# Raw weights of the second batch in two rings and split in pairs, with two sums cut in two steps, in an attention and expert kernel

## The chip, the cores and the metric

One core of a Trainium2 chip runs the whole program. The metric is device time in microseconds (us). The kernel before took 845.05 us (median of three runs, from 843.41 to 851.78); its profiled execution took 843.36 us, of which the span from the first to the last instruction is 841.6 us. Engines are called PE (matmul), PEld (its weight loads), DVE (VectorE), ACT (ScalarE), POOL (GpSimd) and SP (which issues nearly all transfers).

## What is computed

```python
# attention: local window of 16 plus one summary key and value per block of 32; 2 batches, 8 heads, 768 positions
x = attention(q, k, v).reshape(1536, 512)
# first network: 512 -> 2048 -> 512, with a slope alpha per hidden unit
h = x @ w_in
x = (maximum(h, 0) + alpha * minimum(h, 0)) @ w_out
# second network: 4 experts, 512 -> 1024 -> 512, weighted by normalized probabilities p
for e in range(4):
    h = maximum(x @ w1[e], 0)
    out += p[:, e:e + 1] * (h @ w2[e])
```

All of it is float32. Every matmul operand is split into a high part (rounded to PE's fp32r format by an ACT copy) and a low part (operand minus high part, one subtraction on DVE or POOL); a product is three matmuls: high times high, high times low, low times high.

## The kernel before

The program runs attention, then the first network, then the experts; the change touches the experts of the second batch alone. Expert work is cut into 16 **units** per batch, each of two blocks of 128 hidden units (`NQ = 16`), numbered `s` = 0 to 15 for the first batch and 16 to 31 for the second.

The first layer of a unit is a seven-product scheme for 2x2 blocks (`e_steps`, L663). In the order of the work the steps are p1, p2, p6, p5, p7, p4, p3, each of six matmuls with 384 columns. p1, p6, p7 and p4 accumulate in one PSUM tile `cb`, p5 and p3 in `cd`, p2 stands in `ca`. After p1, p6 and p7 an ACT copy saves `cb` (tiles `p` and twice `u`, L669), and the next step on `cb` waits for it: p7 can begin only when the copy `u` after p6 is done. p2 is followed by a DVE addition (`ca`, L696), an ACT high part (`gh`), a DVE low part (`gl`) and an ACT copy for later sums (L686), and these stand ahead of that copy `u` on ACT, which works in order.

The scheme needs sums of both operands. Those of the inputs of batch 1 are the **own sums** (`x_combine`, L608): the blocks B11, B21 and B22 are split first, then four subtractions per half `k` turn the buffer `acc` into T1 to T4 (`own_sums`, on POOL for the second batch), and T1 to T4 are split in turn (`xh`/`xl` for T1, `xeh`/`xel` for the rest). Those of the weights were made and stored in the first batch; a unit of the second batch fetches S1 to S4 ready-made (`e_fetch`) and loads only A11, A12 and A22 raw (`e_load_again`, L470, tile `rc`, 384 KB in two transfers). It splits them in two parts: A11 with A12 (128x512) and A22 (128x256), each one ACT copy and one POOL subtraction (`e_split`, L381). Tile `rc` has one buffer, in the ring `rb` that the second-layer weights of odd units of the first batch use as well.

The second layer of units 16 to 29 is also done by seven products over a pair of units (`l2_quad`), in 21 pieces of six matmuls with 256 columns (`l2q`). Its sums of first-layer results are made on DVE by `s_sums` (four operations per block `f`, tiles `ft`, `fr`, `fe`) and split by `s_split` on ACT and POOL. `paired` weaves a unit's steps with the pieces: its string gives the order, each dot being one piece. After each dot, one entry of `after` runs, into which `e_prep` of the next unit is put: `first` (A11 and A12 split), `last` (A22 split) and `load` (the load for the unit after that), at places given by `at`. Units 15 and below, and 31, go through `standard`.

PE and ACT keep the order in which the code is written; a scheduler orders DVE, POOL and SP. `tc.issue_after(x)` makes it place work behind instruction `x`.

Of the kernel before, what the change touches and what calls it, by code (L numbers as in the profile page):

```python
# [8 lines left out]
F32 = mybir.dt.float32  # L9
# [3 lines left out]
ALU = mybir.AluOpType  # L13
# [79 lines left out]
def kernel(  # L93
# [376 lines left out]
    def e_load_again(s):  # L470
        if s >= 2 * NQ:
            return
        q = s % NQ
        pw["a", s] = t = gp.tile([P, 3, 2 * P], F32, tag="rb", name="rc", bufs=1)
        nc.sync.dma_start(out=t[:, 0:2].rearrange("p a c -> p (a c)"), in_=wb_in[0, 2 * q])
        nc.sync.dma_start(out=t[:, 2], in_=wb_in[0, 2 * q + 1][:, 2 * P:])
# [124 lines left out]
    def x_split(b, name, kk, hi, lo, src):  # L601
        nc.scalar.activation(hi, src, AF.Copy)
        eng = nc.gpsimd if b and name in ("B11", "B21", "B22", "T1") else nc.vector
        eng.tensor_tensor(lo, src, hi.bitcast(F32), op=ALU.subtract)
        for i, k in enumerate(kk):
            xs[b, name, k] = (hi[:, i], lo[:, i]) if len(kk) > 1 else (hi, lo)

    def x_combine(b):  # L608
# [9 lines left out]
        def own_sums(k):  # L618
            b11, b12, b21, b22 = x[:, k, u1], x[:, k, u2], x[:, 2 + k, u1], x[:, 2 + k, u2]
            for y, p, q in ((b11, b12, b11), (b12, b22, b12), (b22, b22, b11), (b21, b21, b22)):  # L620
                (nc.gpsimd if b else nc.vector).tensor_tensor(y, p, q, op=ALU.subtract)
# [102 lines left out]

    def s_sums(s, f):
        a11, a12, a21, a22 = (field(s, n, f) for n in ("A11", "A12", "A21", "A22"))
        nc.vector.tensor_tensor(a22, a21, a22, op=ALU.add)
# [195 lines left out]
    with tc.manual_schedule(engines={mybir.EngineType.PE, mybir.EngineType.Activation}):  # L923
        left, keep = [], []
        l2 = l2_steps(len(units) - 1)[KD // 2:]
        own_at = {NQ - 2: own1, NQ - 1: late1}

        def standard(s, l2, left):
# [3 lines left out]
            if s == NQ - 1:  # L932
                for k in range(2):
                    own_sums(k)
# [9 lines left out]
        def paired(s, order, fill, after=(), at=(2, 6)):  # L944
            fetch, first, last, load = e_prep(s + 1)
            after = list(after) + [lambda: None] * (at[1] - len(after))
            after.insert(at[0], first)
            after[at[1]:at[1]] = [last, load]
# [3 lines left out]
            for x in order:  # L952
# [5 lines left out]
                if s % 2 and quad(s) and x in "43":  # L958
                    s_sums(s, int(x == "4"))
# [8 lines left out]
        for a in range(UA, UB, 2):  # L968
            q = l2_quad(a)
            if old is None:  # L970
                paired(a, "1.26.57...4...3", left + l2, [lambda: None] + last1, (3, 5))
# [4 lines left out]
            else:  # L976
                n = 13 - done
                paired(a, "1.2.6.5.7..4.3" if n == 7 else "1.2.6..5.7..4..3.", old[done:13], splits, (3, 8))
# [8 lines left out]
        paired(UB, "1..2..6...5..7...4...3...", old[done:], splits, (3, 9))  # L987
# [65 lines left out]
```

## Time and profile before

| | before |
|---|---|
| median of the runs (lowest to highest) | 845.05 us (843.41 to 851.78) |
| profiled execution | 843.36 us |
| its span | 841.6 us |
| PE busy | 817.6 us, 97% of the span |
| DVE busy | 608.9 us, 72% |
| ACT busy | 427.3 us, 51% |
| POOL busy | 300.0 us, 36% |
| granted PE clock | full in all of the span but its first slices |

A busy share is an average over stages. The first network ends and the experts begin near 340 us, and the second batch's first unit begins at 583.98 us. A stall is the time for which PE waits between two matmuls. Since matmuls overlap, the time from the start of one to the start of the next tells more than a busy share.

### The profile page before, as it was taken

To read this page: it belongs to the slowest core of one execution; us is meant where nothing else is said; L and a number is where in the kernel's file an instruction comes from. 1 tells how busy PE (TensorE), PEld (TensorE's weight loads), DVE (VectorE), ACT (ScalarE), POOL (GpSimd) and SP (SyncE) were. 2 spreads that over 40 slices of the span, in tenths; PEclk is the share of its full clock that TensorE was granted. 3 is DMA by queue.
4 is the path that set the end of the run, shared out by engine and by line. 5 is a ranking of instruction groups with operands and counts; after the bars stand their busy time and mean duration, and the time that the engine had idled before them with its cause. 6 is when DMAs were issued, how large, how long until landed. Compare 5 with 4: busy or idle time off the path is not lost.

```text
span 841.6 us, 14451 instructions
## 1 busy us (share of the span) xinstructions
PE 817.6 (97%) x5000; PEld 746.0 (89%) x5000; DVE 608.9 (72%) x1313; ACT 427.3 (51%) x1050; POOL 300.0 (36%) x267
## 2 busy tenths in 40 slices
PE   4899999999999999999999999999999999999998
PEld 3699999888888888988989989988899999999997
DVE  7998667999983447477687678685667677767765
ACT  5999995544442334454454454463353554455430
POOL 0000000000013100396796696699153453354330
PEclk9799999999999999999999999999999999999999
DMA  8999413333322100276785785788675766766621
GB/s 310 294 298 298 149 45 102 100 100 101 98 78 75 51 1 0 101 264 225 262 279 215 257 295 196 259 310 294 203 219 188 251 207 213 247 212 227 212 75 75
DMA packets 97496, 155.37 MB, mean 185 GB/s; under 512 B 9872, under 2 KB 48272, under 8 KB 97424
## 3 DMA queue, kind: packets, MB, share of 16 engines
q1 hardware_dynamic: 96848, 154.18, 56.0%
q8 instruction: 39, 0.64, 0.3%
q10 hardware_dynamic: 576, 0.28, 0.1%
q14 instruction: 33, 0.27, 0.1%
HBM read 106.71 MB, written 47.71 MB: 183 GB/s over the span
## 4 chain that ended last, share of the span: by engine, by line
PE 87%; ACT 5%; DMA 4%; DVE 2%; issue 1%; SPq 0%; POOL 0%; ACTq 0%; POOLq 0%
PE l L530 47%; PE cb L646 15%; PE l2q L766 12%; PE cd L646 7%; PE ca L646 3%; ACT sm L232 2%; ACT sm L251 1%; PE s L213 1%; PE pt L257 1%; PE xps L275 1%; DMA bl<-dt 1%; DMA kw<-in_kw 1%; DMA raw<-in_wa 1%; ACT ptb L152 1%; DMA q<-in_qh 1%
## 5 line engine op out<-in xcount | busy, mean ns | idle before, releaser
L385 POOL TENSOR_TENSOR w0l<-ra,w0h 128x256 fp32r<-128x256 f32 (+1 forms) x32 | 36.8, 1151 | 356.8 <-ACT w0h L384 356.8
L813 DVE SCALAR_TENSOR_TENSOR acc<-l,prob_sb,acc 128x512 f32<-128x512 f32 x101 | 74.9, 746 | 28.3 <-PE l L530 28.3
L777 DVE SCALAR_TENSOR_TENSOR acc<-l2q,prob_sb,acc 128x256 f32<-128x256 f32 x156 | 71.0, 478 | 31.3 <-PE l2q L766 29.6
L530 PE MATMUL l<-xh,w0h 128*128 128x512 f32 (+1 forms) x240 | 84.4, 352 | 0.1
L530 PE MATMUL l<-gh,w1h 128*128 128x512 f32 (+1 forms) x240 | 83.3, 350 | 0.0
L530 PE MATMUL l<-xl,w0h 128*128 128x512 f32 (+1 forms) x240 | 83.1, 346 | 0.0
L530 PE MATMUL l<-xh,w0l 128*128 128x512 f32 (+1 forms) x240 | 83.1, 346 | 0.0
L530 PE MATMUL l<-gh,w1l 128*128 128x512 f32 (+1 forms) x240 | 82.9, 347 | 0.0
L530 PE MATMUL l<-gl,w1h 128*128 128x512 f32 (+1 forms) x240 | 81.4, 347 | 0.0
L530 PE MATMUL l<-w1h,gh 128*128 128x512 f32 x192 | 75.5, 393 | 0.0
L530 PE MATMUL l<-w1l,gh 128*128 128x512 f32 x192 | 75.1, 391 | 0.0
L530 PE MATMUL l<-w1h,gl 128*128 128x512 f32 x192 | 75.0, 391 | 0.0
L385 POOL TENSOR_TENSOR w0l<-rc,w0h 128x512 fp32r<-128x512 f32 (+1 forms) x32 | 33.0, 1034 | 80.5 <-ACT w0h L384 66.5
L669 ACT ACTIVATE u<-cb 128x384 f32<-128x384 f32 x64 | 31.3, 490 | 49.2 <-PE cb L646 49.2
L555 DVE SCALAR_TENSOR_TENSOR l<-m,beta,l 128x512 f32<-128x512 f32 (+1 forms) x60 | 38.6, 645 | 23.8 <-ACT m L549 23.7
L549 ACT ACTIVATE m<-l 128x512 f32<-128x512 f32 (+1 forms) x60 | 30.7, 514 | 46.6 <-PE l L530 46.3
L530 PEld LDWEIGHTS l<-xh,w0h 128*128 128x128 f32 x240 | 45.4, 189 | 6.1 <-ACT ptb L152 0.3
L530 PEld LDWEIGHTS l<-gh,w1l 128*128 128x128 f32 x240 | 45.4, 189 | 5.6
L530 PEld LDWEIGHTS l<-gh,w1h 128*128 128x128 f32 x240 | 45.4, 189 | 5.6
L530 PEld LDWEIGHTS l<-xh,w0l 128*128 128x128 f32 x240 | 45.4, 189 | 5.6
L530 PEld LDWEIGHTS l<-xl,w0h 128*128 128x128 f32 x240 | 45.4, 189 | 5.6
L530 PEld LDWEIGHTS l<-gl,w1h 128*128 128x128 f32 x240 | 45.4, 189 | 5.5
(165 smaller groups left out, 2542.3 us busy)
## 6 DMA issues: line engine op xcount, KB each, us to landing
raw<-in_wa SPq DMA_DIRECT2D x32, 512.0 KB, 4.1
rb<-in_wb SPq DMA_DIRECT2D x16, 512.0 KB, 4.8
ra<-in_wb SPq DMA_DIRECT2D x32, 256.0 KB, 3.7
dt<-xh SPq DMA_DIRECT2D x28, 256.0 KB, 3.4
dt<-xl SPq DMA_DIRECT2D x28, 256.0 KB, 4.7
bh<-dt SPq DMA_DIRECT2D x28, 256.0 KB, 3.4
bl<-dt SPq DMA_DIRECT2D x28, 256.0 KB, 3.1
q<-in_qh SPq DMA_DIRECT2D x24, 256.0 KB, 4.8
```

Of the source, the lines that this page charges most:

```text
L152: nc.scalar.activation(dst, src, AF.Copy)
L213: nc.tensor.matmul(sp[:, u], q[:, u // 2, u % 2], kw[:, :, u // 2, u % 2], start=True, stop=True)
L232: nc.scalar.activation(sm[:, u], sm[:, u], AF.Exp, bias=mx[:, u:u + 1], scale=-1.0, accum_out=sume[:, u:u + 1],)
L385: nc.gpsimd.tensor_tensor(lo, src, hi.bitcast(F32), op=ALU.subtract)
L530: ins = nc.tensor.matmul(ps, a, c, start=(i == 0), stop=(i == n - 1))
L549: nc.scalar.activation(m, gs[i, c0][0], AF.Relu, scale=-1.0)
L555: nc.vector.scalar_tensor_tensor(ps, m, beta[:, i:i + 1], ps, op0=ALU.mult, op1=ALU.add)
L646: nc.tensor.matmul(ps, l, r, start=(first and i == 0), stop=(i == len(terms) - 1), skip_group_check=True)
L669: nc.scalar.activation(v[name], ps, AF.Copy)
L766: nc.tensor.matmul(ps, l, r, start=(first and j == 0), stop=(j == len(terms) - 1), skip_group_check=True)
L777: nc.vector.scalar_tensor_tensor(dst, ps, pe, dst, op0=ALU.mult, op1=ALU.add)
L813: nc.vector.scalar_tensor_tensor(acc2[:, t], ps, pe, acc2[:, t], op0=ALU.mult, op1=ALU.add)
```

## The change

It makes five edits. (1) The raw weights of unit 16 are loaded into the ring `raw` (three buffers); the other units keep the one buffer in `rb`. (2) Low parts of B11 and B21 of batch 1 go from POOL to DVE. (3) The own sums come in two steps: the three subtractions per half that make T1, T2 and T3 where all four stood, the one for T4 behind the low parts of T1. (4) In `paired`, A22's split and the next load follow in the gap right behind the split of A11 and A12, at an earlier place than before; unit 18 also has its second piece after p6 ahead of p5. (5) `s_sums` loses its first addition, now `s_first`, which is done at once; the other three for the block `f = 0` are done behind the low part that follows the next unit's p2.

```diff
@@ e_load_again
-        pw["a", s] = t = gp.tile([P, 3, 2 * P], F32, tag="rb", name="rc", bufs=1)
+        if s == NQ:
+            t = wp.tile([P, 3, 2 * P], F32, tag="raw", name="rc", bufs=3)
+        else:
+            t = gp.tile([P, 3, 2 * P], F32, tag="rb", name="rc", bufs=1)
+        pw["a", s] = t
@@ x_split
-        eng = nc.gpsimd if b and name in ("B11", "B21", "B22", "T1") else nc.vector
-        eng.tensor_tensor(lo, src, hi.bitcast(F32), op=ALU.subtract)
+        eng = nc.gpsimd if b and name in ("B22", "T1") else nc.vector
+        low = eng.tensor_tensor(lo, src, hi.bitcast(F32), op=ALU.subtract)
+        if b:
+            mark[name] = low.ins
@@ x_combine
-        def own_sums(k):
+        def own_sums(k, part=None):
             b11, b12, b21, b22 = x[:, k, u1], x[:, k, u2], x[:, 2 + k, u1], x[:, 2 + k, u2]
             for y, p, q in ((b11, b12, b11), (b12, b22, b12), (b22, b22, b11), (b21, b21, b22)):
-                (nc.gpsimd if b else nc.vector).tensor_tensor(y, p, q, op=ALU.subtract)
+                if part is None or part == (y is b21):
+                    (nc.gpsimd if b else nc.vector).tensor_tensor(y, p, q, op=ALU.subtract)
@@
+    def s_first(s, f):
+        nc.vector.tensor_tensor(field(s, "A22", f), field(s, "A21", f), field(s, "A22", f), op=ALU.add)
+
     def s_sums(s, f):
         a11, a12, a21, a22 = (field(s, n, f) for n in ("A11", "A12", "A21", "A22"))
-        nc.vector.tensor_tensor(a22, a21, a22, op=ALU.add)
         nc.vector.tensor_tensor(a21, a11, a21, op=ALU.subtract)
@@ the expert loops
-        own_at = {NQ - 2: own1, NQ - 1: late1}
+        def own_last():
+            with tc.issue_after(mark["T1"]):
+                for k in range(2):
+                    own_sums(k, True)
+
+        own_at = {NQ - 2: own1, NQ - 1: late1 + [own_last]}
@@ standard
             if s == NQ - 1:
                 for k in range(2):
-                    own_sums(k)
+                    own_sums(k, False)
@@ paired
-        def paired(s, order, fill, after=(), at=(2, 6)):
+        def paired(s, order, fill, after=(), at=1):
             fetch, first, last, load = e_prep(s + 1)
-            after = list(after) + [lambda: None] * (at[1] - len(after))
-            after.insert(at[0], first)
-            after[at[1]:at[1]] = [last, load]
+            after = list(after) + [lambda: None] * (at - len(after))
+            after[at:at] = [first, lambda: (last(), load())]
@@
                 if s % 2 and quad(s) and x in "43":
-                    s_sums(s, int(x == "4"))
+                    s_first(s, int(x == "4"))
+                    if x == "4":
+                        s_sums(s, 1)
+                elif x == "2" and s % 2 == 0 and s > UA:
+                    with tc.issue_after(mark[s, 0, 0]):
+                        s_sums(s - 1, 0)
@@
-                paired(a, "1.26.57...4...3", left + l2, [lambda: None] + last1, (3, 5))
+                paired(a, "1.26.57...4...3", left + l2, [lambda: None] + last1, 3)
...
-                paired(a, "1.2.6.5.7..4.3" if n == 7 else "1.2.6..5.7..4..3.", old[done:13], splits, (3, 8))
+                paired(a, "1.2.6..57..4.3" if n == 7 else "1.2.6..5.7..4..3.", old[done:13], splits, 3)
...
-        paired(UB, "1..2..6...5..7...4...3...", old[done:], splits, (3, 9))
+        paired(UB, "1..2..6...5..7...4...3...", old[done:], splits, 3)
```

POOL at the seam of the two batches, from the low part of S1 and S2 of unit 15 on (`w0l<-s`), before. `acc<-acc` is an own subtraction, `xl<-acc` the low part of an input block, `w0l<-rc` that of raw weights of units 16 and 17:

```order
L604 TENSOR_TENSOR xl<-acc,xh 128x2x384 x3
L385 TENSOR_TENSOR w0l<-s_6416,w0h 128x512
L385 TENSOR_TENSOR w0l<-ra,w0h 128x256
L385 TENSOR_TENSOR w1l<-rb,w1h 128x512
L621 TENSOR_TENSOR acc<-acc 128x384 x2
L385 TENSOR_TENSOR w1l<-rb,w1h 128x512
L621 TENSOR_TENSOR acc<-acc 128x384 x5
L385 TENSOR_TENSOR w0l<-rc,w0h 128x512
L385 TENSOR_TENSOR w0l<-rc,w0h 128x256
L621 TENSOR_TENSOR acc<-acc 128x384
L604 TENSOR_TENSOR xl<-acc,xh 128x384 x2
```

The same place now:

```order
L628 TENSOR_TENSOR acc<-acc 128x384 x2
L608 TENSOR_TENSOR xl<-acc,xh 128x2x384
L385 TENSOR_TENSOR w0l<-s_6416,w0h 128x512
L628 TENSOR_TENSOR acc<-acc 128x384
L385 TENSOR_TENSOR w0l<-ra,w0h 128x256
L385 TENSOR_TENSOR w1l<-rb,w1h 128x512
L628 TENSOR_TENSOR acc<-acc 128x384
L385 TENSOR_TENSOR w1l<-rb,w1h 128x512
L628 TENSOR_TENSOR acc<-acc 128x384 x2
L385 TENSOR_TENSOR w0l<-rc,w0h 128x512
L385 TENSOR_TENSOR w0l<-rc,w0h 128x256
L608 TENSOR_TENSOR xl<-acc,xh 128x384 x2
```

Ahead of unit 16's weights there stood seven own subtractions and three wide low parts, and there stand now six and one; the two subtractions for T4 follow behind the last row shown.

DVE around p2 of unit 18, before (`ca<-ca,p` is the addition after p2, `fr`, `fe` are sums of unit 17's results, `acc<-l2q` adds a piece of the second layer):

```order
L730 TENSOR_TENSOR fr<-fr,fe 128x384
L728 TENSOR_TENSOR fr<-fe,fr 128x384
L696 TENSOR_TENSOR ca<-ca,p_7025 128x384
L777 SCALAR_TENSOR_TENSOR acc<-l2q,prob_sb,acc 128x256
L729 TENSOR_TENSOR fe<-ft,fe 128x384
L681 SCALAR_TENSOR_TENSOR gl<-ca,gh 128x384
L730 TENSOR_TENSOR fr<-fr,fe 128x384
```

And now:

```order
L739 TENSOR_TENSOR fr<-fr,fe 128x384
L703 TENSOR_TENSOR ca<-ca,p_7022 128x384
L786 SCALAR_TENSOR_TENSOR acc<-l2q,prob_sb,acc 128x256
L688 SCALAR_TENSOR_TENSOR gl<-ca,gh 128x384
L737 TENSOR_TENSOR fr<-fe,fr 128x384
L786 SCALAR_TENSOR_TENSOR acc<-l2q,prob_sb,acc 128x256
L738 TENSOR_TENSOR fe<-ft,fe 128x384
```

One subtraction went from before the addition after p2, and one from before its low part, to behind that low part.

ACT from the end of unit 18 to the copy `u` after p6 of unit 19, before:

```order
L686 ACTIVATE ft<-cd 128x384
L734 ACTIVATE xh<-fr 128x384
L384 ACTIVATE w0h<-rc 128x256
L669 ACTIVATE p_7197<-cb 128x384
L680 ACTIVATE gh<-ca 128x384
L686 ACTIVATE fe<-ca 128x384
L384 ACTIVATE w0h<-rc 128x512
L669 ACTIVATE u_7248<-cb 128x384
```

And now:

```order
L693 ACTIVATE ft<-cd 128x384
L743 ACTIVATE xh<-fr 128x384 x2
L676 ACTIVATE p_7197<-cb 128x384
L687 ACTIVATE gh<-ca 128x384
L693 ACTIVATE fe<-ca 128x384
L384 ACTIVATE w0h<-rc 128x512
L384 ACTIVATE w0h<-rc 128x256
L676 ACTIVATE u_7255<-cb 128x384
```

The 128x256 copy ahead of `p` (unit 19's A22) has left this stretch for one behind p7 of unit 18; the one now ahead of `u` is unit 20's A22, whose 128x512 copy stood there before as well.

## Rows read from the trace of the kernel before

**Rows 1.** The page: span, then busy us (share) xinstructions of each engine.

```profile
span 841.6 us, 14451 instructions
PE 817.6 (97%) x5000; PEld 746.0 (89%) x5000; DVE 608.9 (72%) x1313; ACT 427.3 (51%) x1050; POOL 300.0 (36%) x267
```

**Rows 2.** Waits of PE, 350 to 841 us: us in total, times, longest.

```profile
PE cb L646 <- ACT u L669: 3.2, 3, 1.4
PE cb L646 <- POOL w0l L385: 0.7, 1, 0.7
PE cd L646 <- DVE gl L681: 0.3, 1, 0.3
```

**Rows 3.** Stretches, line 646: length, PE busy (x), PEld busy (x), clock, DMA share, GB/s.

```profile
568.47:575.77 7.30, 7.30 (x42) 7.14 (x41) 1.00 0.72 217
583.98:594.30 10.32, 8.14 (x42) 7.02 (x41) 1.00 0.72 263
```

**Rows 4.** Stretches, PE alone: length, PE busy (x), clock, DMA share, GB/s.

```profile
619.75:625.18 5.43, 4.84 (x33) 1.00 0.66 176
633.62:640.57 6.95, 5.57 (x38) 1.00 0.71 215
664.88:670.16 5.28, 5.28 (x39) 1.00 0.88 262
668.40:669.11 0.71, 0.71 (x7) 1.00 0.79 231
```

**Rows 5.** Timeline at the seam: start us, length us, instruction, [idle before <-releaser].

```profile
578.36 5.22 POOL L621 TENSOR_TENSOR acc<-acc 128x384 f32<-128x384 f32 x5
578.90 0.39 SPq L475 DMA_DIRECT2D rc<-in_wb  x1
583.11 0.94 ACT L384 ACTIVATE w0h<-rc 128x512 fp32r<-128x512 f32 x2 [5.43 <-DMA rc<-in_wb]
583.82 1.98 POOL L385 TENSOR_TENSOR w0l<-rc,w0h 128x512 fp32r<-128x512 f32 x2 [0.24 <-ACT w0h L384]
```

**Rows 6.** Chain of waits, 583 to 594.6 us: start us, us, what.

```profile
585.32 3.47 DVE xel L604 x3
...
590.55 0.48 DVE ca L696
...
592.62 0.49 ACT u L669
```

**Rows 7.** Timeline around unit 18's p2.

```profile
619.10 2.62 POOL L735 TENSOR_TENSOR xl<-ft,xh 128x384 fp32r<-128x384 f32 x2
619.47 1.37 DVE L728 TENSOR_TENSOR fr<-fe,fr 128x384 f32<-128x384 f32 x1
620.76 0.55 DVE L696 TENSOR_TENSOR ca<-ca,p 128x384 f32<-128x384 f32 x1
623.47 0.48 ACT L669 ACTIVATE u<-cb 128x384 f32<-128x384 f32 x1
```

**Rows 8.** Timeline in unit 19.

```profile
634.23 0.33 SPq L475 DMA_DIRECT2D rc<-in_wb  x1
635.28 0.49 ACT L686 ACTIVATE fe<-ca 128x384 f32<-128x384 f32 x1 [0.68 <-DVE gl L681]
638.33 0.63 ACT L384 ACTIVATE w0h<-rc 128x512 fp32r<-128x512 f32 x1 [2.56 <-DMA rc<-in_wb]
```

**Rows 9.** Line 604, low parts of inputs: ns min/median/max, first and last start, forms.

```profile
L604 DVE TENSOR_TENSOR xel<-acc,xeh x12: 550/556/1370, 324.8 to 597.1; 128x384 fp32r<-128x384 f32 x12
L604 DVE TENSOR_TENSOR xl<-acc,xh x5: 552/958/958, 300.1 to 328.9; 128x768 fp32r<-128x768 f32 x3, 128x384 fp32r<-128x384 f32 x2
L604 POOL TENSOR_TENSOR xl<-acc,xh x5: 1323/1840/1847, 566.6 to 588.3; 128x768 fp32r<-128x768 f32 x3, 128x384 fp32r<-128x384 f32 x2
```

**Rows 10.** Timeline in unit 17: its copy after p6 and its p7.

```profile
609.85 0.48 ACT L669 ACTIVATE u<-cb 128x384 f32<-128x384 f32 x1
610.98 0.33 PE L646 MATMUL cb<-xeh,wfh 128*128 128x384 f32 x1
```

## The prediction

> **What bounds the kernel now.** I read the page first. PE is busy for 817.6 of 841.6 us [rows 1], so other engines matter only where PE waits for them. The whole idle time is 24 us. Of it, only what lies in the expert stage, which begins behind 340 us, can be touched, and there the waits of PE [rows 2] are five in all, three of them for the ACT copy `u` that saves the PSUM tile between p6 and p7 (3.2 us), one for the low part of unit 16's raw weights (0.7), one for a DVE low part (0.3). Nothing else in that stage stops PE. So the change can give at most what these five stalls cost, and the rest of my work is to price each and ask whether its cause goes.
>
> A wait as listed is less than the cost of a stall, because matmuls overlap and the first after a pause runs longer. I therefore compare stretches with the same matmuls. Unit 15's seven steps take 7.30 us for 42 matmuls; the 42 from unit 16's p1 to its p7 (two steps of unit 15 among them) take 10.32 [rows 3]. The **seam** costs 3.02 us: the wait for the raw weights, the one for DVE and one for `u`. From p6 to the end of p7 unit 21 takes 5.28 us; unit 19, with the same steps and pieces, 6.95 [rows 4], so its stall costs 1.67. Unit 18 has one piece fewer in that stretch, and one takes 0.71, so 5.28 - 0.71 = 4.57 is due; it takes 5.43 and loses 0.86. Together 3.02 + 0.86 + 1.67 = **5.55 us** can be gained.
>
> **The seam, raw weights (edits 1 to 3).** Unit 16's load is issued at 578.90 and ACT gets it at 583.11 after 5.43 us of waiting [rows 5], since its one buffer belongs to unit 15's second-layer weights until POOL has split them. In the ring `raw` it takes a buffer last used by unit 14, which is a whole unit (583.98 - 568.47 = 15.5 us, rows 3) earlier: the wait of ACT goes. That alone is worth nothing, as POOL is late too: its five own subtractions end at 578.36 + 5.22 = 583.58, 0.24 before the low part starts [rows 5]. Now two wide low parts (1.84 each on POOL, rows 9) and one own subtraction (5.22 / 5 = 1.04) leave the queue ahead of it, 4.72 us, so POOL could start at 583.82 - 4.72 = 579.1.
>
> Against that stand waits between POOL and DVE. DVE's subtraction of two SBUF tiles takes 0.55 us alone and up to 1.37 [rows 9]; three took 3.47 while POOL ran [rows 6], 1.16 each. DVE gets two more of the wide kind (0.96 each, rows 9), and the four narrow ones come earlier, into POOL's busy time. If POOL stood still for all of them it would lose 2 x 0.96 + 4 x 0.55 = 4.1 us and start at 583.2; if for none, at 579.1. PE wants the low part with p1's third matmul, about 584.3, and it takes 1.3 of the 1.98 of both. Cost left: nothing to 0.2 us. I take nothing. The first own subtraction also waits for DVE's low part of B11, which falls in the same bounds.
>
> **The seam, p5 and p7 of unit 16.** p7 needs `u`, and ACT, in order, does `u` behind the work on p2's result, which starts with DVE's `ca`. That came at 590.55 because DVE was working on T2 and T3 (`xel`, 3.47 us from 585.32, when ACT's copies had come at last) [rows 6]. From the end of `ca` (591.03) to the end of `u` (593.11) are 2.08 us. Without stalls p2 ends three steps after 583.98, at 587.10 (a step is 7.30 / 7 = 1.04), and p7 is due three steps later, 3.12. So `ca`, 0.55 long [rows 7], must begin within 0.5 us of p2's end. ACT's copies of T2 and T3 now wait for the own subtractions alone, which end between 579.1 and 583.2; with 0.9 for two copies (0.94 in rows 5) the three `xel` run from 580 to 584 to 583.5 to 587.6, and additions to `acc` that queued behind them follow. At the early end DVE is free in time; at the late end most of the old loss stays. I take the middle, 581 for POOL, at which `ca` is just in time or some tenths late: 0.2 us left, between 0 and the 2.0 or so that the seam lost there (3.02 less the 0.7 of rows 2 and its slow restart).
>
> Here a rule speaks against the change. The rows just read show DVE's two-input subtractions more than doubled beside POOL. The Trainium skill (SBUF — State Buffer, "Who interferes with whom") says that a DVE instruction with two SBUF inputs and a GpSimd instruction that reads SBUF exclude each other for a whole instruction. By that rule none of the moved low parts is hidden under POOL's work, and the first rival below would be likelier than I make it; without it the first bound, 0, would stand.
>
> **Unit 18 (edit 5, and the piece ahead of p5).** `ca` came at 620.76, right behind a subtraction for the sums that took 1.37 while POOL ran; `u` ended at 623.95 [rows 7], and p7 was due at 619.75 [rows 4] + 2 x 1.04 + 2 x 0.71 = 623.25. That subtraction now stands behind `gl`, and so does the next. `ca` then moves up by between 0.55 (the subtraction alone; its slow part could pass to the one before) and 1.3 us, and `gl` by the next subtraction's 0.55 more at best: `u` ends between 622.1 and 623.4. Left: 0 to 0.15, I take 0. The piece ahead of p5 needs the low parts `xl<-ft` 1.04 us earlier; POOL finished them at 621.72 [rows 7], and its 128x256 low part no longer stands before them. PE comes to that piece at 621.50 and to the first low part two short matmuls later, so even at the old times it loses next to nothing. The sums of `f = 0` that come later feed pieces that are several steps off.
>
> **Unit 19 (edit 4).** ACT stood from 635.77 to 638.33 before the copy of unit 20's weights, with `u` behind it; the load was issued at 634.23, so it took 4.1 us [rows 8]. Its call now stands in unit 18 two pieces and two steps earlier, 2 x 0.71 + 2 x 1.04 = 3.5 us: issue at 630.7 or earlier, there at 634.8, 1 us before ACT wants it. Left: nothing to the whole 1.67; I take nothing.
>
> **What else moves.** In units of odd number A22's copy (128x256) now stands ahead of `u`, and in unit 17 the 128x512 copy too (0.63 us, rows 8). Unit 17 has the least cover: `u` ended at 610.33 and p7 began at 610.98 [rows 10], 0.65 of slack for 0.63; without it 0.1 us would be lost. Edit 4 issues no transfer more; unit 16's goes out earlier, among others that use the queue at a DMA share of 0.72 [rows 3]; nothing waits there within a microsecond. PE's own instructions are the same.
>
> **Sum.** 5.55 - 0.2 = 5.35 us off the profiled execution's 843.36: 838.0. Before, the median of the runs stands 1.7 above that execution, the lowest run at it; I put the median at **838.5 us**.
>
> **Rivals.**
> - *The port.* DVE and POOL hold each other up at the seam so that `ca` is as late as before. For it: rows 6 and 9. Against it: 4.72 us less in POOL's queue. 2 us of the gain stay out: 840 to 841.
> - *The load is early for nothing.* SP issues it late, or POOL alone decides: the whole seam stays, and units 18 and 19 gain 2.53: 841.
> - *Slower.* The one buffer for raw weights is now asked for earlier in every unit, and ACT, in order, meets its copies earlier. If the transfer is not there when ACT reaches it in an odd unit, `u` waits, as unit 19 showed for 1.67 us. It decides from the point where the transfer lands later than the copy `fe` ends; for unit 19 I found 1 us of room. Units 19 to 29 are six odd units with the same order: 838.0 + 6 x 1.67 = 848 us, slower than before. Against it: later units had no such stall, the load has moved up further than its use, and a transfer takes some 4 us where a unit takes 15.
> - *More than the five stalls.* PE would have to run the same matmuls faster; nothing in the change touches that.
>
> **Chances.** My forecast 0.65; the port 0.17; the early load for nothing 0.08; slower 0.05; other 0.05. The measurement of this kernel tells about 1% from no change, 8.4 us. My forecast, at 0.8%, is within it and so are all rivals; faster by more needs a median below 836.6, which takes all 5.55 us and lucky runs, 0.08; slower by over 1% needs more than the slower rival, 0.03; 0.89 for the rest. The range runs from 836.6 (all stalls gone, the runs close to the profiled one) to 842.3 (the port or the seam left as it is, with the runs' usual 1 to 2 us above the profiled execution).
>
> **What would show it.** Right: no wait of PE for `u` in units 18 and 19, the stretch from unit 16's p1 to its p7 near 7.5 us, ACT without a wait for `rc`, POOL's low part of unit 16's weights before 583. Wrong: `ca` of unit 16 starting over 0.5 us after p2's last matmul with `xel` or additions ahead of it; PE at p1 of unit 16 still waiting for POOL; a wait for `rc` on ACT in odd units; a wait at the piece ahead of p5 in unit 18.

## The result, and the profile after

| | before | after |
|---|---|---|
| median of 5 runs, us | 845.23 (843.41, 845.05, 845.23, 851.43, 851.78) | 838.82 (837.62 to 839.05) |
| profiled execution, us | 843.36 | 838.46 |
| its span, us | 841.6 | 836.7 |
| waits of PE behind 345 us | 4.2 | none |

The ratio is 0.9896 (0.9848 to 0.9944), which is that of the means of the five runs, 838.57 and 847.38 us. That is a gain of 1.04%, and its interval excludes no change. The medians differ by 6.41 us, 0.76%, where 0.8% was forecast, and the time lies 0.3 us from the forecast. With 0.89 on "within 1%", that part of the prediction failed.

Between the two profiled executions the steps did what the forecast said. These are stretches of line 653 (646 before) and of PE alone in the changed kernel; the columns are those of [rows 3] and [rows 4], and each stretch ends where the next matmul starts, as there.

```profile
584.59:591.90 7.31, 7.30 (x42) 7.14 (x41) 1.00 0.82 299
```

```profile
617.39:621.96 4.57, 4.57 (x33) 1.00 0.29 93
630.40:635.68 5.28, 5.28 (x39) 1.00 0.79 253
```

The 42 matmuls of the seam take 7.31 us after 10.32, p6 to p7 of unit 18 takes 4.57 after 5.43, and of unit 19 5.28 after 6.95. That is 3.01 + 0.86 + 1.67 = 5.54 us (forecast 5.35): all that the five stalls cost. The spans differ by 4.9 only, since the changed kernel's execution comes 0.65 us later to the first expert matmul, ahead of all that the change touches. Here it is before, then after:

```profile
336.19 0.33 PE L646 MATMUL cb<-xh,w0h 128*128 128x384 f32 x1
336.84 0.33 PE L653 MATMUL cb<-xh,w0h 128*128 128x384 f32 x1
```

From there to the end, the **expert part**, the execution before took 505.4 us and the one after 499.8. The timeline of the seam (start us, length us, instruction) answers to [rows 5] and [rows 6]:

```profile
578.20 0.92 ACT L384 ACTIVATE w0h<-rc 128x512 fp32r<-128x512 f32 x2
578.65 0.55 DVE L688 SCALAR_TENSOR_TENSOR gl<-c,gh 128x384 fp32r<-128x384 f32 x1
581.01 2.63 POOL L385 TENSOR_TENSOR w0l<-rc,w0h 128x512 fp32r<-128x512 f32 x2
582.06 3.29 DVE L608 TENSOR_TENSOR xel<-acc,xeh 128x384 fp32r<-128x384 f32 x3
...
587.94 0.57 DVE L703 TENSOR_TENSOR ca<-ca,p 128x384 f32<-128x384 f32 x1
...
590.11 0.49 ACT L676 ACTIVATE u<-cb 128x384 f32<-128x384 f32 x1
```

ACT no longer waits for `rc`. POOL starts on it at 581.01 (taken: 581). `ca` starts 0.2 after p2 gives way to the next step (587.74), and `u` is there 0.26 before p7 starts (590.86). For unit 19, against [rows 8], the load of unit 20's weights leaves at 625.47 (at 630.7 or earlier, said the forecast), and ACT finds it landed:

```profile
632.05 0.49 ACT L693 ACTIVATE fe<-ca 128x384 f32<-128x384 f32 x1 [0.68 <-DVE gl L688]
632.44 0.93 ACT L384 ACTIVATE w0h<-rc 128x512 fp32r<-128x512 f32 x2
633.27 0.48 ACT L676 ACTIVATE u<-cb 128x384 f32<-128x384 f32 x1
```

What the two traces do not explain is the comparison: its two runs of the kernel before above 851 us stand 6 to 8 us above its others, and there is no such stall in [rows 2]. Without these two the mean before would be 844.56 us and the gain 6.0 us, 0.7%.

### The profile page after: what moved, and what is told of

Read it like the earlier page. It is cut to its first block, busy times and chain, and to the rows that moved or that the text cites. A ratio compares the mean times of both kernels' runs of the same rounds, so it can differ in the third digit from the quotient of the medians.

```text
span 836.7 us, 14449 instructions
## 1 busy us (share of the span) xinstructions
PE 814.9 (97%) x5000; PEld 745.1 (89%) x5000; DVE 614.5 (73%) x1315; ACT 428.3 (51%) x1050; POOL 294.6 (35%) x265
## 4 chain that ended last, share of the span: by engine, by line
PE 92%; ACT 4%; DMA 2%; DVE 1%; issue 0%; ACTq 0%; SPq 0%
PE l L534 48%; PE cb L653 16%; PE l2q L775 13%; PE cd L653 8%; PE ca L653 4%; PE s L213 2%; ACT sm L232 1%; DMA kw<-in_kw 1%; ACT sm L251 1%; PE xps L275 1%; PE pt L257 1%; DMA alpha_sb<-in_alpha 1%; ACT ptb L152 1%; ACT xh L152 0%; ACT m L553 0%
## 5 line engine op out<-in xcount | busy, mean ns | idle before, releaser
L385 POOL TENSOR_TENSOR w0l<-s,w0h 128x512 fp32r<-128x512 f32 x32 | 47.9, 1515 | 2.9 <-ACT w0h L384 2.9
```

Source lines behind the costliest of these rows:

```text
L385: nc.gpsimd.tensor_tensor(lo, src, hi.bitcast(F32), op=ALU.subtract)
```

## The experiments

Behind each expectation stand the median in us and the ratio to the kernel before in the same comparison, with its 95% interval. There are five comparisons besides the one above. The kernel before had a median of 843.56 in the first comparison (24 runs), 843.06 in the second (35), 844.48 in the third (35), 843.24 in the fourth (17), 849.51 in the fifth (23).

### What each edit is worth

**Edits 1 to 3 taken back** (unit 16's `rc` from the one buffer, low parts of B11 and B21 on POOL, own sums in one step).

```
-        if s == NQ:
-            t = wp.tile([P, 3, 2 * P], F32, tag="raw", name="rc", bufs=3)
-        else:
-            t = gp.tile([P, 3, 2 * P], F32, tag="rb", name="rc", bufs=1)
-        pw["a", s] = t
+        pw["a", s] = t = gp.tile([P, 3, 2 * P], F32, tag="rb", name="rc", bufs=1)
...
-        eng = nc.gpsimd if b and name in ("B22", "T1") else nc.vector
+        eng = nc.gpsimd if b and name in ("B11", "B21", "B22", "T1") else nc.vector
...
-        own_at = {NQ - 2: own1, NQ - 1: late1 + [own_last]}
+        own_at = {NQ - 2: own1, NQ - 1: late1}
...
-                    own_sums(k, False)
+                    own_sums(k)
```

> The changed kernel with edits 1 to 3 taken back (unit 16's raw weights in their old ring, low parts of B11 and B21 on POOL, all own sums in one step); edits 4 and 5 stay. Theory (five separate stalls, each owned by its edits): the stretch from unit 16's p1 to the start of what follows its p7 is 10.3 us again and units 18 and 19 stay without a stall: the span is 3.0 us above the changed kernel's. Rival (the stalls are linked: what unit 16 loses is made up later or brings the others back): the span differs by under 1 us or over 4.5 us.

840.67; ratio 0.9963 (0.9947 to 0.9980). PE waited 0.4 us for `w0l` and 0.9 for one `u` at the seam, and nowhere else. The expert part takes 501.7 us, 1.9 more than in the changed kernel: less than the theory's 3.0 and more than the rival's 1, so neither holds as it stands.

**Edit 4 and the piece ahead of p5 taken back** (the same at the other calls of `paired`).

```
-            after[at:at] = [first, lambda: (last(), load())]
+            after.insert(at[0], first)
+            after[at[1]:at[1]] = [last, load]
...
-                paired(a, "1.2.6..57..4.3" if n == 7 else "1.2.6..5.7..4..3.", old[done:13], splits, 3)
+                paired(a, "1.2.6.5.7..4.3" if n == 7 else "1.2.6..5.7..4..3.", old[done:13], splits, (3, 8))
```

> The changed kernel with edit 4 taken back (places of the splits and of the load in the gaps, and the order of unit 18's piece and p5, as before). Theory: the load for unit 20 is issued some 9 us later, ACT waits 2 to 3 us for it in unit 19, the stretch from p6 to the end of p7 there is 6.95 us instead of 5.28 and the span is 1.7 us above the changed kernel's; unit 18 stays at 4.57. Rival (the sums alone, edit 5, cured both units): unit 19 stays at 5.28 and the span is the same.

839.39; 0.9960 (0.9940 to 0.9979). One wait of PE is left, 1.1 us for `u` of unit 19, behind ACT's wait for the load, as in [rows 8]. Unit 19's stretch takes 6.62 us (6.95 expected), and the expert part 1.4 us more than in the changed kernel (1.7 expected). One of the 12 runs took 848.40.

```profile
630.52 0.33 SPq L479 DMA_DIRECT2D rc<-in_wb  x1
```

```profile
634.31 0.63 ACT L384 ACTIVATE w0h<-rc 128x512 fp32r<-128x512 f32 x1 [2.27 <-DMA rc<-in_wb]
634.85 0.47 ACT L676 ACTIVATE u<-cb 128x384 f32<-128x384 f32 x1
```

**Edit 5 taken back.**

```
-                    if x == "4":
-                        s_sums(s, 1)
-                elif x == "2" and s % 2 == 0 and s > UA:
-                    with tc.issue_after(mark[s, 0, 0]):
-                        s_sums(s - 1, 0)
+                    s_sums(s, int(x == "4"))
```

> The changed kernel with edit 5 taken back (all four sums of a block at once). Theory: the addition after p2 of unit 18 comes again behind a subtraction of the sums, PE waits for the copy u before p7, and the stretch from p6 to the end of p7 is 5.4 us instead of 4.57; later even units have 0.57 us of room and stay without a stall: 0.9 us on the span. Rival (the longer subtraction in unit 18 came from POOL's 128x256 low part, which edit 4 moved away): unit 18 stays near 4.6.

839.85; 0.9951 (0.9935 to 0.9967). One wait of PE, 1.0 us for `u` of unit 18, whose stretch takes 5.82 us (5.4 expected). The slow subtraction stands ahead of `ca` again, as in [rows 7]:

```profile
616.42 1.12 DVE L739 TENSOR_TENSOR fr<-fr,fe 128x384 f32<-128x384 f32 x1
617.46 1.37 DVE L737 TENSOR_TENSOR fr<-fe,fr 128x384 f32<-128x384 f32 x1
618.76 0.55 DVE L703 TENSOR_TENSOR ca<-ca,p 128x384 f32<-128x384 f32 x1
```

**The kernel before, and the changed kernel, once more**, with no edit.

> The kernel before, unchanged, profiled and timed once more, for the spread of its runs (843.4 to 851.8 us) against that of the changed kernel (837.6 to 839.1). Theory (the change saves five fixed stalls and nothing else): the profile has the same five stalls of 5.5 us in sum, and runs near 851 differ from those near 844 in a part of the program that the change leaves alone. Rival (the runs near 851 lose time in the second batch's experts, where a transfer of raw weights sometimes lands late, and the change takes that away as well): a run or profile above 848 shows more or longer waits of PE for u, and the changed kernel and its variants with edit 4 have no run so far above their lowest.

842.53; 0.9984 (0.9972 to 0.9997). Its profiled execution (841.69 us) has the same waits, smaller: 2.5 us for `u`, 0.4 for `w0l`, none for `gl`, and its expert part takes 503.8 us, 4.0 more than in the changed kernel. The five stalls are no fixed 5.55 us. No run of this comparison lay above 847, so what the runs near 851 are stayed open.

> The changed kernel, unchanged, on one chip with more runs of the kernel before. Theory (the change is worth its five stalls, 4 to 5.5 us, and the first comparison's ratio of 0.990 came from a sample of the kernel before in which two runs of five stood near 851 us): no wait of PE in the second batch's experts, median 838 to 839 us, ratio 0.993 to 0.995. Rival (the change is worth over 1%, by something that the profiled executions do not show): ratio 0.991 or below against a larger sample.

839.44; 0.9959 (0.9937 to 0.9981), no wait of PE in the experts. The gain is a little smaller than the theory had it, from a kernel before of which 3 of 35 runs lay above 847. One of the 12 runs took 846.01.

**Edit 1 alone taken back** (the first six lines of the first diff above).

> The changed kernel with edit 1 alone taken back: unit 16's raw weights again in the one-buffer ring. Theory: the load is issued near 579 us, ACT waits some 5 us for it with its copies of T1 to T3 behind, PE waits for the raw weights' low part in p1 (0.5 to 0.9 us) and for u before p7 (0.5 to 1.2 us): 1.3 to 2 us on the seam. Rival (POOL alone decided, so that a shorter POOL queue is enough): under 0.5 us.

842.89; 0.9992 (0.9973 to 1.0012): the whole gain is gone, more than the 1.3 to 2 us expected and more than with edits 1 to 3 back together. In the profiled execution, the slowest of the 12 (844.93), ACT waits 4.63 us for `rc`, and everything queued behind it, T2 and T3 among it, is late; PE waits 1.0 us for `gl` and 1.2 for `u`, and then its granted clock falls to the lower level (1.2 GHz). The stretches show length, then the busy time of PE, PEld, DVE, ACT and POOL, and the clock ahead of the last two columns:

```profile
584.97 0.94 ACT L384 ACTIVATE w0h<-rc 128x512 fp32r<-128x512 f32 x2 [4.63 <-DMA rc<-in_wb]
```

```profile
591.00:595.60 4.60, 2.50 (x13) 1.85 (x11) 3.60 (x7) 1.32 (x4) 1.82 (x2) 1.00 0.89 279
595.60:599.10 3.50, 3.40 (x10) 3.12 (x11) 1.52 (x3) 1.32 (x4) 0.00 (x0) 0.51 0.06 22
```

**Edit 3 alone taken back** (the last four lines of that diff).

> The changed kernel with edit 3 alone taken back: all eight own subtractions where six stand. Theory: POOL reaches unit 16's weights one or two subtractions later (1.0 to 2.1 us), 582 to 583, early enough for p1; T2 and T3 come later by up to 1 us and p7 loses 0 to 0.8 us. Rival (edit 3 is needed as much as the other two): over 1 us on the seam.

839.15; 0.9946 (0.9922 to 0.9970), as the changed kernel, with 0.2 us of wait for `w0l`. Edit 3 is worth nothing that can be measured.

**Half of edit 4**: A22 split early, the load back at its old step.

```
-            after[at:at] = [first, lambda: (last(), load())]
+            after[at[1]:at[1]] = [load]
+            after[at[0]:at[0]] = [first, last]
...
```

> The changed kernel, with one half of edit 4 kept and the other taken back: A22 of the next unit is split at its new, early place, but the load of the raw weights behind it goes back to its old number of steps, on SP's queue behind two or four transfers of unit parts that themselves wait for a buffer. Theory (place in the queue): in unit 18 the load for unit 20 is then issued near 634 to 635 instead of 625.5, ACT waits 2 us or more for it in unit 19 as it did before, and PE loses 1.2 to 1.7 us there: 839.8 to 841 against 839.4. Rival (the split was what mattered): the buffer came free late because A22 was split late, so with the early split the load goes out in time wherever it stands, no wait of ACT, and the time is the changed kernel's, 838.8 to 839.6.

839.04; 0.9922 (0.9888 to 0.9957). The rival held: no wait of PE, and in unit 18 the load goes out at 626.80, in an execution that runs 1.3 us later than the one above. In this unit no transfer of SP's lies between the load's two places, so there the buffer's release through A22's early split did it alone; in the other units the load went later past two transfers, and that cost nothing.

**The piece ahead of p5 alone taken back.**

```
-                paired(a, "1.2.6..57..4.3" if n == 7 else ...
+                paired(a, "1.2.6.5.7..4.3" if n == 7 else ...
```

> The changed kernel with the piece ahead of p5 of the units of even number back between p5 and p7. Theory: p7 of unit 18 is due at the same time either way, since only the order of p5 and of one piece ahead of it changes, and the wait for u was removed by edit 5 alone: no stall of PE in units 18 and 19, 838.8 to 839.6, the same as the changed kernel. Rival: the piece covers part of the wait for u in unit 18, and a stall of 0.3 to 0.9 us comes back there: 839.7 to 840.3.

838.83; 0.9923 (0.9890 to 0.9956), no wait of PE. Worth nothing, as the theory had it; unit 18's stall went with edit 5.

**Edits 1 and 2 alone, in the kernel before.**

```
+        if s == NQ:
+            t = wp.tile([P, 3, 2 * P], F32, tag="raw", name="rc", bufs=3)
...
-        eng = nc.gpsimd if b and name in ("B11", "B21", "B22", "T1") else nc.vector
+        eng = nc.gpsimd if b and name in ("B22", "T1") else nc.vector
```

> The kernel before with the ring and the low parts of B11 and B21 changed (edits 1 and 2), the other edits not made. Theory (the edits add up, and the seam needs these two): the seam's stalls go but for some tenths at p1 (0.2 to 0.5 us), the one of unit 18 (0.8 to 1.3) and the one of unit 19 (1.2 to 1.7) stay; 1.3 to 2.6 us off the kernel before, a median of 840.7 to 842. Rival (the edits help each other): without edit 4 and the string the seam's gain of 1.8 us shows only in part, and the median is within 0.7 us of the kernel before. As to the kernel before, whose 59 runs in two calls gave medians of 843.56 and 843.06 with three runs at or above 847.8: I expect 842.5 to 844 again, with no more than one run in ten above 847.

842.62; 0.9968 (0.9939 to 0.9997). The seam is clear but for 0.2 us; `u` of units 18 and 19 stays, 2.3 us. None of its 12 runs lies above 843.79; the median misses the expected 842 by 0.6. The kernel before's own runs scatter here from 840.44 to 853.23. Of those, 14 of 35 lay above 847, where one in ten was expected: the question became what these are.

### The runs of the kernel before near 850 us

**Edit 2 alone taken back** (the two lines with `eng` of the first diff) gave the first sign.

> The changed kernel with edit 2 alone taken back: low parts of B11 and B21 on POOL again. Theory: POOL's queue grows by 2 x 1.84 = 3.7 us less what DVE no longer takes from it (up to 1.4), so it reaches unit 16's weights near 583.5 instead of 581.0 and the own subtractions end as much later: up to 0.6 us at p1 and 0.5 to 1.2 at p7. Rival (the port: on DVE these two held POOL up for as long as they took there): POOL reaches the weights at the same time, within 0.5 us, and the seam stays without a stall.

848.13; 1.0044 (1.0019 to 1.0069), slower than before; ten of 12 runs at 846.3 to 851.5, the other two at 841.58 and 841.70. Neither the theory (up to 1.8 us lost) nor its rival (nothing lost) foresaw it. In its trace `gl<-c`, the low part of the last block of unit 15's results, which DVE makes from two SBUF tiles, takes 10.51 us where it took 0.55 above. PE waits 7.8 us for the DVE addition queued behind it, which reads a PSUM tile `l` that PE is to write again:

```profile
577.36 10.51 DVE L688 SCALAR_TENSOR_TENSOR gl<-c,gh 128x384 fp32r<-128x384 f32 x1
```

**The same, with POOL made to wait once.** One POOL instruction more reads that `gl`, ahead of the low part of unit 16's weights.

```
+            if (s, f, half) == (NQ - 1, 1, 1):
+                w = gp.tile([P, TP], F32, tag="m", name="w", bufs=MBUFS)
+                mark["w"] = nc.gpsimd.tensor_tensor(w, gl.bitcast(F32), gl.bitcast(F32), op=ALU.subtract).ins
...
+            if s == NQ:
+                with tc.issue_after(mark["w"]):
+                    pair = e_split(pool, 0, src, len(names) * 2 * P)
```

> The changed kernel with edit 2 back (the low parts of B11 and B21 on POOL), as in the run that took 848.13 us and in whose profile one DVE instruction of unit 15, gl<-c with its two SBUF inputs, took 10.51 us while POOL worked without a pause; and, new, one POOL instruction more (128x384, about 1.0 us) in POOL's queue ahead of the low part of unit 16's raw weights, which reads that gl and so makes POOL wait until DVE has done it. Theory (starved): POOL's unbroken queue kept DVE from its second SBUF input, and the 8 us pause of PE, with the halved clock after it, was only that. Then POOL's pause lets DVE through at 580 to 580.5 at the latest, gl<-c takes 1 to 3 us, no matmul step of unit 15's second layer is longer than 2 us, the clock keeps its upper level, and the run costs the changed kernel's time plus what POOL's queue is longer (two low parts and the new instruction, 4.7 us, less what cover there is): 840.5 to 843.5, though work was added. Rival (the queue's length): POOL was simply 3.7 us later in all it did at the seam, and with one more instruction the median is 848 or more. Rival (the DVE instruction itself): gl<-c is slow whatever POOL does, and stays near 10 us.

842.23; 0.9957 (0.9922 to 0.9991), none of 12 above 845.3: with work added, 5.9 us less than without the wait (in another comparison). What is left above the changed kernel is 2.3 us of waiting for `p`, since T2 and T3 come later. In its trace, however, DVE got through at the end of POOL's running instruction (0.96 us), so that the wait made the difference is shown by the times alone.

**The kernel before, unchanged, for its trace.**

> The kernel before, unchanged, for its trace. Theory (starved): if the profiled execution takes over 847 us, its trace shows one of unit 15's or 16's DVE instructions with two SBUF inputs taking over 3 us while POOL works without a pause, PE waiting behind it for 3 us or more, and a stretch at half clock after that; if it takes 841 to 845, no such instruction over 1.5 us in these units and no half-clock stretch there. Rival (another cause): an execution over 847 us whose DVE instructions in units 15 and 16 all take under 1.5 us, with its loss somewhere else or spread over the span.

> The kernel before, unchanged, for its trace, as in the run ahead of this: over 847 us goes with a starved DVE instruction of over 3 us in units 15 and 16 and a stretch at half clock after it (theory), or with neither (rival); 841 to 845 us with neither.

> The kernel before, unchanged, for its trace, as in the two runs ahead of this: over 847 us goes with a starved DVE instruction of over 3 us in units 15 and 16 and a stretch at half clock after it (theory), or with neither (rival); 841 to 845 us with neither.

> The kernel before, unchanged, for its trace and the count. One of the three looks (843.73 us) had a DVE gl<-c of 5.67 us in unit 15, PE standing 3.0 us behind it, and no half-clock stretch after it. Theory: an execution over 847 us is this with a half-clock stretch after it (as in the run with the low parts on POOL, where 10.51 us of starvation were followed by 10.24 us at half clock); 3 in 10 to 1 in 20 of its runs above 847, none of the kernel in which POOL waits. Rival: over 847 us without a starved DVE instruction.

Three of these executions took 844.58, 842.67 and 843.73, and the fourth 850.92. The first two have no starved instruction (`gl<-c` took 0.92 and 0.79 us). The third has one, where the expectation had none for 841 to 845 us; PE waits 3.0 us behind it and keeps its clock. The timeline of DVE, then of POOL, then the wait of PE and the stretch that holds it:

```profile
577.95 5.67 DVE L681 SCALAR_TENSOR_TENSOR gl<-c,gh 128x384 fp32r<-128x384 f32 x1
583.55 2.06 DVE L813 SCALAR_TENSOR_TENSOR acc<-l,prob_sb,acc 128x512 f32<-128x512 f32 x3
```

```profile
577.10 1.29 POOL L385 TENSOR_TENSOR w1l<-rb,w1h 128x512 fp32r<-128x512 f32 x1
578.35 4.85 POOL L621 TENSOR_TENSOR acc<-acc 128x384 f32<-128x384 f32 x5
583.33 2.13 POOL L385 TENSOR_TENSOR w0l<-rc,w0h 128x512 fp32r<-128x512 f32 x2
```

```profile
PE l L530 <- DVE acc L813: 3.0, 1, 3.0
```

```profile
581.00:584.90 3.90, 0.90 (x4) 0.48 (x3) 3.90 (x4) 2.28 (x6) 3.78 (x5) 1.00 0.92 267
```

POOL paused from 583.20 to 583.33, and `gl` ended at 583.62. In the fourth, ACT's copy of `rc` was there in time and POOL had no such pause:

```profile
578.32 10.53 DVE L681 SCALAR_TENSOR_TENSOR gl<-c,gh 128x384 fp32r<-128x384 f32 x1
588.78 2.05 DVE L813 SCALAR_TENSOR_TENSOR acc<-l,prob_sb,acc 128x512 f32<-128x512 f32 x3
```

```profile
577.57 1.28 POOL L385 TENSOR_TENSOR w1l<-rb,w1h 128x512 fp32r<-128x512 f32 x1
578.82 4.86 POOL L621 TENSOR_TENSOR acc<-acc 128x384 f32<-128x384 f32 x5
583.64 1.95 POOL L385 TENSOR_TENSOR w0l<-rc,w0h 128x512 fp32r<-128x512 f32 x2
585.54 0.99 POOL L621 TENSOR_TENSOR acc<-acc 128x384 f32<-128x384 f32 x1
586.49 1.94 POOL L604 TENSOR_TENSOR xl<-acc,xh 128x384 fp32r<-128x384 f32 x2
```

The queue ended at 588.43 and `gl` at 588.85. Its waits of PE, the matmul that waited, and four stretches:

```profile
PE l L530 <- DVE acc L813: 7.9, 1, 7.9
PE cb L646 <- ACT u L669: 1.9, 2, 1.3
```

```profile
589.57 0.80 PE L530 MATMUL l<-w1h,gh 128*128 128x512 f32 x1 [7.86 <-DVE acc L813]
```

```profile
580.00:584.10 4.10, 1.71 (x8) 1.09 (x6) 4.10 (x1) 2.10 (x6) 4.10 (x5) 1.00 0.88 263
584.50:588.30 3.80, 0.00 (x0) 0.00 (x0) 3.80 (x1) 0.91 (x3) 3.80 (x5) 0.50 0.29 108
588.30:593.00 4.70, 3.43 (x8) 2.77 (x9) 2.99 (x5) 0.00 (x0) 0.14 (x1) 0.50 0.00 0
594.40:599.00 4.60, 4.60 (x27) 4.53 (x26) 2.59 (x5) 1.32 (x3) 0.00 (x0) 1.00 0.90 292
```

PE stands still for 7.9 us, loses the upper clock level meanwhile and starts again at the lower. The seam's small stalls are gone in this execution, since everything else has caught up. 850.92 is 7.8 above the 843.09 that is the median of the kernel before's runs below 847.

**The kernel before with POOL made to wait once**, by the same extra instruction, ahead of the own subtractions; twice. One of the five subtractions moves behind the low part of unit 16's weights, so that POOL has as much to do ahead of that as before.

```
+            if (s, f, half) == (NQ - 1, 1, 1):
+                w = gp.tile([P, TP], F32, tag="m", name="w", bufs=MBUFS)
+                g = gl.bitcast(F32)
+                mark["w"] = nc.gpsimd.tensor_tensor(w, g, g, op=ALU.subtract).ins
...
+            if s == NQ - 1:
+                with tc.issue_after(mark["w"]):
+                    for k in range(2):
+                        own_sums(k, (1, 2, 3))
```

> The kernel before with one POOL instruction more (128x384, about 1 us): it reads the gl<-c of unit 15 and stands in POOL's queue behind unit 15's last second-layer weights and ahead of the own subtractions, so POOL must wait there until DVE has done that gl; one own subtraction of the five moves behind the low part of unit 16's weights, so the queue ahead of that is as long as before. Theory (starved, in the kernel before too): the runs of the kernel before near 850 us, 14 of 35 above 847 in the last comparison, 3 of 35 and none of 24 in the two earlier ones, are those in which DVE's gl<-c did not get through POOL's five subtractions in a row. With POOL made to wait they are gone: the highest of 12 runs lies below 847.5, the median at 842 to 844.5, whatever share of the kernel before's own runs in this comparison lies above 847. Rival (another cause: the chip, the clock, the memory): the share above 847 is the same in both kernels, and where the kernel before has a third of its runs there, so has this. If the kernel before has no such run in this comparison, it tells nothing.

> The kernel before with POOL made to wait once for unit 15's gl<-c, again, for the count of its runs above 847 us: none of 12 the first time, beside 2 of 17 of the kernel before. Theory (starved): none of 12 again, highest below 847.5. Rival (another cause): as large a share above 847 as the kernel before has in this comparison.

843.83 and 843.30; 0.9996 (0.9971 to 1.0021) and 0.9938 (0.9907 to 0.9969). None of its 24 runs lies above 845.91. The kernel before has 2 of 17 and 14 of 23 above 847 in the same two comparisons, and so have 9 of the 12 runs to which the fourth execution belongs. In both profiled executions POOL now waits 0.49 us for `gl<-c`, which is through in 0.79 and 0.95 us; of the second:

```profile
578.72 0.95 DVE L688 SCALAR_TENSOR_TENSOR gl<-c,gh 128x384 fp32r<-128x384 f32 x1
```

```profile
579.75 0.83 POOL L695 TENSOR_TENSOR w<-gl 128x384 f32<-128x384 f32 x1 [0.49 <-DVE gl L688]
```

What the edit changes is POOL's unbroken queue, and the place of one own subtraction with it. The starvation theory holds, and a disturbance from outside, which would have hit both kernels, does not explain these runs.

## Why the prediction was right and where it failed

**The steps held**, on the execution that they were worked out from.
- *Seam, raw weights and p5/p7*: 3.01 us of the 3.02 that it cost, where 2.82 was forecast; POOL at 581.01, `ca` 0.2 late, nothing lost. That POOL came within a hundredth of the 581 taken is luck: the bounds 579.1 and 583.2 were worked out, and between them the middle was taken. Edit 1 and edit 2 are each needed: with one of the two back the kernel is at 842.89 or 848.13. Edit 3 is not.
- *Unit 18*: all 0.86, by edit 5; the piece ahead of p5 adds nothing.
- *Unit 19*: all 1.67, by the early split of A22 that frees the buffer. The reason given was another, the place of the load's call, worth 3.5 us; the load left 8.8 us earlier, and half of edit 4 shows that its place is not what counts.
- *What else moves*: unit 17's `u` ended at 608.45 and p7 began at 608.58, 0.13 of slack, where the forecast left 0.02 (0.65 less 0.63).
- *Rivals*: neither the port as I meant it (`ca` late) nor the load early for nothing nor late loads came about. But DVE and POOL did hold each other up: `xel` still took 3.29 us for three, 1.10 each against 0.55 alone.

**The step that failed** stands under "Chances": "The measurement of this kernel tells about 1% from no change, 8.4 us", from which 0.89 went to no change that could be told. Nothing in the prediction works this figure out, and it was too wide. The interval of the comparison on record reaches 0.48% to either side, 4 us, so the forecast gain of 0.8% was itself clear of no change. In the second of the later comparisons a gain of 0.41% was clear as well (0.9937 to 0.9981).

**A second step failed** under "What bounds the kernel now", and it carried the gain past 1%: "the change can give at most what these five stalls cost". It took one profiled execution for all. In that execution the bound held, 5.54 of 5.55 us. In the second profiled execution of the kernel before the stalls cost 4.0, and some runs held a stall that this one did not have. Of the 139 runs of the kernel before in the six comparisons, the 104 below 847 have a median of 843.09, the other 35 one of 850.72, and 851.78 was one of the three times on show. I read it as scatter and worked out no mechanism for it. The profiled execution held the sign, in a row of its timeline that I had not looked for:

```profile
578.03 0.79 DVE L681 SCALAR_TENSOR_TENSOR gl<-c,gh 128x384 fp32r<-128x384 f32 x1
```

This took 0.79 us, not 0.55, as it came through between two POOL instructions. The rival "more than the five stalls" was dismissed because nothing makes the same matmuls run faster; it needed only a stall that the profiled execution did not have.

So the gain has two parts. From the runs below 847 the change takes off 843.09 - 839.17 (the median of the changed kernel's 17 runs) = 3.9 us, 0.5%; from the others some 11.5 us. The border is one of times: the execution of 843.73 us was starved too, for less long. The comparison on record, with two runs near 851 in five, showed 1.04%, and 0.7% without them. That the medians' 0.76% lies so near the 0.8% forecast is in part luck: both count from a median of a few runs, 845.23 and 845.05, where the 104 below 847 have 843.09. With 14 of 35 the third of those above gave 0.8% for two versions that do as well as the changed kernel, and with none of 24 and 3 of 35 the first two gave 0.4 to 0.5%.

**Why the change removes the starvation** is shown in part: it goes with edit 2 and comes back, worse, without it. Of the 94 runs of the changed kernel and of the seven versions that keep edit 2, one lies above 847; of the kernel before's 99 in the same four comparisons, 19. Edit 2 with no other edit was not run, and the version with edits 1 to 3 back tells nothing (none of 7, beside none of 24). In both executions of the changed kernel and in the seven versions that keep edit 2, `gl<-c` started 0.13 to 0.26 us before the end of POOL's running `w1l`, and took 0.55 to 0.68. In the executions with the old order 0.37 to 0.55 was left. With 0.39 or less all got through; the three that were starved had 0.44 to 0.54. But two others with 0.50 and 0.55 left, behind which POOL worked on without a pause, got through with the wait for that one instruction (0.92 and 0.96 us). What decides there is open. So is why its share differs so much between comparisons (none of 24 to 14 of 23; they ran on several chips, and what the chip does to it was not tested), and whether the changed kernel's one run at 846.01 and one of 848.40 with edit 4 back are the same: they weren't profiled.

## What to carry to other kernels

A run that stands 1% above the others is a second behaviour of the kernel until shown otherwise: before a sum is made from one profile, look for the instruction whose duration is not its own even there, and ask what it would cost if the wait went on. Where DVE's result gates PE, keep its two-SBUF-input instructions from starting under a long unbroken queue of POOL, or let POOL wait once: an instruction of 0.8 us took away a loss of 8. An early load needs everything ahead of it moved together: a ring without the queue behind it (edit 1 without 2) was worse than no change. And work out from the scatter of the runs how small a gain a comparison can tell, before calling one too small.

## What the runs showed of the hardware

- DVE's two-SBUF-input instruction, started under a POOL instruction, ended 0.41 to 0.42 us behind that one's end in 17 of 20 profiled executions (0.79 us with 0.37 left), and the POOL instruction after it takes 1.33 instead of 1.01. Starved, it waited through six POOL instructions (5.67 us) or eleven (10.53, 10.51), which ran unhindered (an own subtraction every 0.97 us), and ended 0.41 to 0.42 behind the last of them. The Trainium skill (SBUF — State Buffer, "Who interferes with whom") says that issue order decides who blocks; by its "Summary: rules for kernel authors" the second to issue "fully blocks" until the first finishes. The usual case agrees; the starved one goes beyond it, as DVE was passed over at five to ten boundaries.
- A pause of POOL of 0.13 us was enough to let DVE in (843.73 us run).
- PE's granted clock stayed at its upper level (2.4 GHz) through a wait of 3.0 us (843.73 us run) and was at the lower (1.2 GHz) from about 584.2 to 594.4 around one of 7.9. In that stretch a 128x512 matmul step took 427 ns instead of 227.
- Executions of the same instructions come to unit 15 up to 1.3 us apart in the kernel before (`gl<-c` at 577.95 to 579.26), and with them the first expert matmul, at 336.10 to 337.53 (`gl<-c` follows it by 241.7 to 241.9): a scatter from ahead of the experts, which no edit at the seam touches.
